# A written order of VectorE, ScalarE and GpSimd for the first block of the second MoE layer, with one weight piece a half

## Chip, cores and metric

One NeuronCore of one Trainium2 chip runs the kernel. The metric is device time in microseconds (us), the median of several runs. Engines: PE is TensorE, DVE is VectorE, ACT is ScalarE, POOL is GpSimd, SP is SyncE, which issues the DMAs here.

## The reference

A windowed attention (with 32 global tokens) is followed by two MoE layers on its 2176 output tokens (4 x 544):

```python
x = attention(q_l, k_l, v_l, q_g, k_g, v_g)      # 2176 tokens x 512
x = layer_norm(solu(x @ w1_in)) * g_ln @ w1_out   # 512 -> 1024 -> 512
h = x @ w2_in                                     # 512 -> 2048
g = where(h >= 1, h, where(h <= -1, 0, (h + 1)**2 / 4))
out = g @ w2_out                                  # 2048 -> 512
```

The inputs `w2_in` and `w2_out` arrive as 64-bit floats. The kernel turns each into two 32-bit numbers, a high and a low part whose sum is the weight, on the chip. Every product is made of three matmuls (high x high, high x low, low x high), which keeps the precision.

## The kernel before

**Stages.** Attention and the first MoE layer come first, up to 309 us. The second layer runs over three blocks of tokens: block 0 (6 tiles of 128 tokens), block 1 (6) and block 2 (5). Its 2048 columns are 16 pieces `f` of 128: for each there is an "i" weight piece (of `w2_in`) and an "o" weight piece (of `w2_out`).

**Block 0, a loop over f = 1 to 15 (line 1084).** A block's tokens are two halves of 384 columns. In this text half k = 2f + (0 or 1). In each half PE makes `h` (`h2`, line 673: 12 matmuls of 384 columns into one PSUM bank of a pool of three, one of which an accumulator takes for good after the first halves), and then 9 matmuls of 512 columns that add piece f - 2 into the six PSUM accumulators (`accum`, line 703; three tiles a half). The activation of a half is `bend` and `least` (lines 688 to 694), then a split in two parts:

- ACT: `relu` (`xy<-h`), then `square` (`xy<-xy`);
- DVE: `least` (`xy<-h,xy`, a minimum and maximum of PSUM and SBUF), after which the PSUM bank is free for the half after next;
- ACT: the high part (`g<-xy`); POOL: the low part (`g<-xy,g`, one instruction of 384 columns).

**A weight piece** is a DMA of 512 KB into one of three buffers `wraw` (`fetch`, line 213) and seven steps (`conv`, line 164): A on ACT (`w<-wraw`), C and B on DVE (`w<-w`), D and F on DVE (`w<-wraw,w`, lines 178 and 180; after F the buffer `wraw` is free), H on ACT (high part, `wo<-w` or `lnT<-w`) and L (low part: DVE here). At the loop's start 19 of the 32 pieces are left. The loop converts two pieces before an odd f and one before an even f (`weights(1 + f % 2, vec)`, line 1086), both pieces step by step together. The "o" pieces live in five rotating buffers (`WO = 5`): piece o(f) takes the buffer of o(f - 5). Each "o" piece is also stored to DRAM (`store_out`) for blocks 1 and 2. `order2` (line 230) sorts the pieces: i(f) by f, o(f) by f + 4.

**What sets the order.** PE and SP follow the written order of the program. In block 0 DVE, ACT and POOL are ordered by the framework's scheduler, within the dependencies (`vec.gate` adds a few). In blocks 1 and 2 (line 1101 on) all engines follow the written order.

**Blocks 1 and 2** make two pieces f at once (`pair`, line 802) by seven products of half the depth (products 0 to 6, of 6 matmuls each) and sums of their results: DVE forms `u1` after product 1 and `u2` after product 3 (lines 829 and 831), and product 4 writes the bank that `u2` reads. The products need sums of weights (`wfull` on POOL, `wsum` on DVE, `whigh` on ACT, `wlow` on POOL, tile `S`) and sums and splits of the tokens (`ysum` on DVE, `yhigh` on ACT, `ylow` on DVE or POOL; tiles `yc` and `yT`). Those that the first pairs of block 1 need are listed in `early` (line 1078) in iterations f = 12 to 15; the scheduler may pull them forward.

**The end of a block.** After the last piece `finish` (line 869) copies each accumulator to SBUF (`o<-acc`, even tiles on ACT, odd ones on DVE) and stores it. Accumulators 0 and 1 are one PSUM tile, 2 and 3 another. A tile is copied right behind its own last matmul, and the framework lets the matmuls of the other accumulator of the same PSUM tile wait for that copy.

## Time and profile before

| | us |
|---|---|
| median of 3 runs | 699.83 |
| the three runs | 699.63, 699.83, 703.38 |
| the profiled execution's own time | 698.82 |
| its span in the trace | 697.0 |
| PE busy | 661.3 (95% of the span) |
| PEld busy | 574.0 (82%) |
| DVE busy | 449.1 (64%) |
| ACT busy | 350.7 (50%) |
| POOL busy | 256.4 (37%) |
| mean granted clock of PE | 0.991 |

The span is what the trace covers; the own time has what lies around it (1.8 us). PE is busy nearly always, but not evenly: the idle time lies at the start, in block 0, at the entry into block 1 and at the very end. In block 0 PE is the engine that all wait for only in some halves, so a share over the whole span says little there.

### The profile page before, as it was taken

To read this page: it belongs to the slowest core of one execution; us is meant where nothing else is said; L and a number is where in the kernel's file an instruction comes from. 1 tells how busy PE (TensorE), PEld (TensorE's weight loads), DVE (VectorE), ACT (ScalarE), POOL (GpSimd) and SP (SyncE) were. 2 spreads that over 40 slices of the span, in tenths; PEclk is the share of its full clock that TensorE was granted. 3 is DMA by queue.
4 is the path that set the end of the run, shared out by engine and by line. 5 is a ranking of instruction groups with operands and counts; after the bars stand their busy time and mean duration, and the time that the engine had idled before them with its cause. 6 is when DMAs were issued, how large, how long until landed. Compare 5 with 4: busy or idle time off the path is not lost.

```text
span 697.0 us, 15054 instructions
## 1 busy us (share of the span) xinstructions
PE 661.3 (95%) x6095; PEld 574.0 (82%) x6095; DVE 449.1 (64%) x800; ACT 350.7 (50%) x859; POOL 256.4 (37%) x275
## 2 busy tenths in 40 slices
PE   5799899999999999999999989989999999999996
PEld 3467788988898898998787778978888888989984
DVE  5999999988777499539755674355555544333332
ACT  4887574354563255344644445544544466444443
POOL 3343633112112143034222247376677645222220
PEclk9999999999999999999999999999999999999999
DMA  8979557435355333002553341555333356644512
GB/s 347 394 257 398 206 185 269 165 127 186 123 217 153 150 92 121 1 0 75 198 151 121 123 149 62 187 171 185 121 121 122 120 182 211 233 130 152 196 46 77
DMA packets 29398, 113.71 MB, mean 163 GB/s; under 512 B 3472, under 2 KB 3984, under 8 KB 26768
## 3 DMA queue, kind: packets, MB, share of 16 engines
q1 hardware_dynamic: 29184, 112.48, 46.0%
q8 instruction: 48, 0.79, 0.5%
q10 hardware_dynamic: 144, 0.26, 0.1%
q14 instruction: 22, 0.18, 0.1%
HBM read 88.87 MB, written 23.86 MB: 162 GB/s over the span
## 4 chain that ended last, share of the span: by engine, by line
PE 67%; DVE 18%; DMA 7%; ACT 3%; issue 3%; POOL 0%; SPq 0%; ACTq 0%; DVEq 0%
PE acc L267 19%; PE h L267 17%; PE h L512 11%; PE yT L267 10%; DVE w L178 3%; DMA wraw<-in_w2o_dram 3%; DVE w L180 3%; DMA wraw<-in_w2i_dram 2%; DVE xy L138 2%; PE S L343 2%; PE plnT L561 2%; PE o L415 2%; PE pPT L400 2%; DVE w L174 1%; DVE e L138 1%
## 5 line engine op out<-in xcount | busy, mean ns | idle before, releaser
L267 PE MATMUL acc<-wo,g 128*128 128x512 f32 x816 | 212.7, 394 | 1.8 <-ACT o L147 1.8
L162 POOL TENSOR_TENSOR g<-xy,g 128x384 fp32r<-128x384 f32 (+1 forms) x95 | 97.2, 1029 | 207.1 <-ACT g L147 163.8
L267 PEld LDWEIGHTS acc<-wo,g 128*128 128x128 f32 x816 | 150.1, 189 | 26.4 <-ACT o L147 2.7
L147 ACT ACTIVATE xy<-xy 128x384 f32<-128x384 f32 (+1 forms) x144 | 72.5, 504 | 71.2 <-DVE xy L138 67.1
L512 PE MATMUL h<-win,x 128*128 128x512 f32 x408 | 102.7, 401 | 0.2 <-DVE x L500 0.2
L267 PE MATMUL yT<-lnT,wout 128*128 128x256 f32 x768 | 94.9, 281 | 0.0
L267 PEld LDWEIGHTS yT<-lnT,wout 128*128 128x128 f32 x768 | 92.3, 188 | 0.8
L512 PEld LDWEIGHTS h<-win,x 128*128 128x128 f32 x408 | 74.4, 188 | 16.8 <-DVE x L500 0.7
L138 DVE TENSOR_TENSOR xy<-h,xy 128x384 f32<-128x384 f32 (+1 forms) x64 | 33.5, 523 | 59.6 <-PE h L267 59.1
L267 PE MATMUL h<-yT,w2i 128*128 128x384 f32 (+1 forms) x300 | 58.6, 342 | 7.1 <-DVE xy L138 4.5
L267 PEld LDWEIGHTS h<-yT,w2i 128*128 128x128 f32 x300 | 52.2, 191 | 13.6 <-DVE xy L138 9.5
L138 DVE SCALAR_TENSOR_TENSOR xy<-h,xy 128x384 f32<-128x384 f32 (+1 forms) x48 | 26.0, 541 | 55.8 <-ACT xy L147 55.8
L147 ACT ACTIVATE g<-xy 128x384 fp32r<-128x384 f32 (+1 forms) x96 | 47.8, 498 | 27.8 <-DVE xy L138 27.6
L147 ACT ACTIVATE xy<-h 128x384 f32<-128x384 f32 (+1 forms) x64 | 30.0, 469 | 51.9 <-PE h L267 51.8
L267 PE MATMUL h<-yT,S 128*128 128x384 f32 (+1 forms) x288 | 54.7, 325 | 0.0
L147 ACT ACTIVATE e<-S,nm 128x128 f32<-128x128 f32 x128 | 45.0, 384 | 18.4 <-DVE nm L138 18.4
L267 PEld LDWEIGHTS h<-yT,S 128*128 128x128 f32 x288 | 48.3, 188 | 5.4 <-DVE xy L138 1.9
L172 ACT ACTIVATE w<-wraw 128x512 f32<-128x512 f32 x33 | 22.1, 673 | 35.4 <-DMA wraw<-in_w2o_dram 21.9
L547 POOL TENSOR_TENSOR rstd<-rstd,nhalf 128x1 f32<-128x1 f32 x17 | 10.8, 633 | 79.1 <-DVE rstd L138 67.6
L267 PE MATMUL h<-yT,lnT 128*128 128x384 f32 (+1 forms) x180 | 34.9, 339 | 5.2 <-DVE xy L138 5.2
L267 PEld LDWEIGHTS h<-yT,lnT 128*128 128x128 f32 x180 | 31.0, 188 | 10.0 <-DVE xy L138 9.2
L500 POOL TENSOR_TENSOR x<-xy,x 128x512 fp32r<-128x512 f32 x16 | 20.7, 1294 | 42.7 <-ACT x L147 42.7
(135 smaller groups left out, 1044.3 us busy)
## 6 DMA issues: line engine op xcount, KB each, us to landing
wo<-w2d_o SPq DMA_DIRECT2D x33, 512.0 KB, 3.3
vw<-in_vwin_dram SPq DMA_DIRECT2D x16, 1024.0 KB, 8.5
qkT<-in_qk_dram SPq DMA_DIRECT2D x16, 832.0 KB, 6.8
wraw<-in_w2i_dram SPq DMA_DIRECT2D x16, 512.0 KB, 4.3
wraw<-in_w2o_dram SPq DMA_DIRECT2D x16, 512.0 KB, 3.9
w2d_s<-S SPq DMA_DIRECT2D x16, 512.0 KB, 5.5
S<-w2d_s SPq DMA_DIRECT2D x16, 512.0 KB, 5.9
w2d_o<-wo SPq DMA_DIRECT2D x15, 512.0 KB, 5.7
```

Of the source, the lines that this page charges most:

```text
L138: self.last = getattr(nc.vector, name)(*args, **kw)
L147: vec.act = nc.scalar.activation(**kw)
L162: eng.tensor_tensor(out=lo, in0=src, in1=hi.bitcast(F32), op=ALU.subtract)
L172: return nc.scalar.activation(out=w.tf, in_=w.high.bitcast(F32), func=AF.Abs)
L178: return nc.vector.scalar_tensor_tensor(out=w.t, in0=w.high, scalar=-0x40000000, in1=w.t, op0=ALU.bitwise_and, op1=ALU.bitwise_or)
L180: return nc.vector.scalar_tensor_tensor(out=w.t, in0=w.low, scalar=29, in1=w.t, op0=ALU.logical_shift_right, op1=ALU.bitwise_or)
L267: mm(out=dst, lhsT=pairs[i][0][x], rhs=pairs[i][1][y], start=start and j == 0, stop=stop and j == 3 * n - 1, **kw)
L343: mm(out=S[32 * hp:32 * hp + 32, par, ci], lhsT=qT[r, hp, ci], rhs=kT[r, hp, w:w + 4].rearrange("p c d -> p (c d)"), start=True, stop=True)
L400: nc.tensor.transpose(ps[:, hp], eT[t][:, HP * par + hp], ident)
L415: mm(out=o[rows, ci, par], lhsT=PT[t][:, par, ci, rows], rhs=w[:, ci, D * h:D * h + D], start=True, stop=True)
L500: eng.tensor_tensor(out=xT[t][1], in0=x[:, :, n:n + P], in1=xT[t][0].bitcast(F32), op=ALU.subtract)
L512: mm(out=hps[t][:, half], lhsT=x[i][:, k], rhs=win[j][:, k, sl], start=not lo and j == 0 and k == 0, stop=lo and k == KD - 1)
```

## The change

- In block 0 too, DVE, ACT and POOL follow a written order. The loop runs over the halves k = 2 to 31 (the first two stand before it). In each half, the order is: `h` on PE; `relu` and `square`; L of the piece before last and C of the last piece on DVE; `least`; A of a new piece on ACT (none in halves 11 and 21, `REST`); B, D, F of the last piece on DVE; the high part of `g`; its low part on POOL, now two instructions of 192 columns; H of the last piece on ACT; the `early` steps of this half; then the 9 accumulating matmuls.
- `order2` sorts o(f) by f + 6 instead of f + 4. All stashed pieces are now "i" pieces, 19 pieces are left for the loop as before, and in the loop the last seven (o9 to o15, halves 15 to 22) follow each other without an "i" piece between them.
- `early` is spread over the halves 24 to 31. The weight sums that block 1 needs first (`wfull`, `wsum`, `whigh`, `wlow`) stand in halves 26 to 31.
- In the first pair of block 1, `yhigh` stands ahead of the other extra steps of its product and `ylow` one product later.
- `finish` copies accumulators 0 and 1 together when both are complete, and 2 and 3 likewise. At the very end accumulator 2 of block 2 is copied by DVE instead of ACT, ahead of accumulator 3 on ACT.

```diff
+REST = (11, 21)
-    order2 = [... for f in range(K2)] + [(f + 4, "o", f) for f in range(K2)])]
+    order2 = [... for f in range(K2)] + [(f + 6, "o", f) for f in range(K2)])]
...
-        lasts = {j: f for f, j in order}
-        return [lambda f=f, j=j: step(f, j, lasts[j] == f) for f, j in order]
+        lasts = {j: (f, j) for f, j in order}
+        done = {at: [] for at in order}
+        for j in range(n):
+            both = [lasts[i] for i in {j, j ^ 1} if i < n and max(j, i) < 4] or [lasts[j]]
+            done[max(both, key=order.index)].append(j)
+        return [lambda f=f, j=j: step(f, j, done[f, j]) for f, j in order]
...
-        if i % 2:
+        if i % 2 or (b, i) == (len(BLOCKS) - 1, 2):
...
-        weights2(16, in_lnr)
+        weights2(18, in_lnr)
-        vec.gate = True
         early = {
-            K2 - 4: [yhigh(1, 0), ylow(1, 0), ysum(1, 0)],
-            K2 - 3: [ysum(1, 1), yhigh(1, 2), ylow(1, 2), ysum(1, 2)],
-            K2 - 2: [yhigh(1, 1), ylow(1, 1), ysum(1, 3)],
-            K2 - 1: [wfull(0, 0), wfull(0, 1), wsum(0, 0..3), whigh(0), wlow(0, 0), wlow(0, 1), wfull(1, 0), wfull(1, 1)],
+            (12, 0): [yhigh(1, 0), ylow(1, 0)],
+            (12, 1): [ysum(1, 0), yhigh(1, 2), ylow(1, 2)],
+            (13, 0): [ysum(1, 1), wfull(0, 0)],
+            (13, 1): [ysum(1, 2), yhigh(1, 1), wfull(0, 1)],
+            (14, 0): [ysum(1, 3), ylow(1, 1)],
+            (14, 1): [wsum(0, 0..3)],
+            (15, 0): [whigh(0), wlow(0, 0), wlow(0, 1)],
+            (15, 1): [wfull(1, 0), wfull(1, 1)],
         }
-        for f in range(1, K2):
-            store_out(3)
-            weights(1 + f % 2, vec)
-            fetch(3 - len(fetched))
-            h2(0, f, 0)
-            if f >= 2:
-                accum(0, f - 2, range(3))
-            h2(0, f, 1)
-            if f >= 2:
-                accum(0, f - 2, range(3, len(BLOCKS[0])))
-            for op in early.get(f, ()):
-                op()
         with tc.manual_schedule(engines={DVE, Activation, Pool}):
+            for k in range(2, 2 * K2):
+                f, half = divmod(k, 2)
+                if half == 0:
+                    store_out(3)
+                fetch(3 - len(fetched) - (piece_now is not None))
+                h, s, gh, gl = hprod(0, f, half)
+                bend(h, s)
+                if piece_low:
+                    conv("L", piece_low, vec)
+                if piece_now:
+                    conv("C", piece_now)
+                least(h, s)
+                piece_next = None
+                if fetched and k not in REST:
+                    make, raw, scale = fetched.pop(0)
+                    piece_next = word(make(), raw, scale)
+                    conv("A", piece_next)
+                if piece_now:
+                    for step in "BDF":
+                        conv(step, piece_now)
+                act(out=gh, in_=s, func=AF.Copy)
+                m = s.shape[1] // 2
+                for sl in (slice(0, m), slice(m, 2 * m)):
+                    sub(gl[:, sl], s[:, sl], gh[:, sl].bitcast(F32), nc.gpsimd)
+                if piece_now:
+                    conv("H", piece_now)
+                piece_low, piece_now = piece_now, piece_next
+                for op in early.get((f, half), ()):
+                    op()
+                if f >= 2:
+                    accum(0, f - 2, range(3) if half == 0 else range(3, len(BLOCKS[0])))
...
-                                extra[i] += [yhigh(1, 3 + i), ylow(1, 3 + i, nc.gpsimd if i % 2 else vec)]
+                                extra[i].insert(0, yhigh(1, 3 + i))
+                                extra[i + 1].insert(0, ylow(1, 3 + i, nc.gpsimd if i % 2 else vec))
```

**DVE in the middle of block 0.** In these rows `h2_...` is the PSUM bank of a half (its row is `least`), `w32_...` a piece in work, `wraw_...` its raw words. Rows of the scalar kind with one `w32` are C, then B; those with `wraw` are D, then F; the last kind is L. Before, f = 9 and 10:

```order
L138 SCALAR_TENSOR_TENSOR xy0_88<-h2_5132,xy0_88 128x384
L174 TENSOR_SCALAR w32_5160<-w32_5160 128x512
L174 TENSOR_SCALAR w32_5162<-w32_5162 128x512
L176 TENSOR_SCALAR w32_5160<-w32_5160 128x512
L176 TENSOR_SCALAR w32_5162<-w32_5162 128x512
L178 SCALAR_TENSOR_TENSOR w32_5160<-wraw_5035,w32_5160 128x512
L178 SCALAR_TENSOR_TENSOR w32_5162<-wraw_5037,w32_5162 128x512
L180 SCALAR_TENSOR_TENSOR w32_5160<-wraw_5035,w32_5160 128x512
L180 SCALAR_TENSOR_TENSOR w32_5162<-wraw_5037,w32_5162 128x512
L138 SCALAR_TENSOR_TENSOR xy0_88<-h2_5180,xy0_88 128x384
L138 TENSOR_TENSOR wo_5159<-w32_5160,wo_5159 128x512
L138 TENSOR_TENSOR lnT1_87<-w32_5162,lnT0_86 128x512
```

And with the change, halves 18 and 19 (the same place in the program):

```order
L177 TENSOR_SCALAR w32_5183<-w32_5183 128x512
L141 SCALAR_TENSOR_TENSOR xy0_88<-h2_5207,xy0_88 128x384
L179 TENSOR_SCALAR w32_5183<-w32_5183 128x512
L181 SCALAR_TENSOR_TENSOR w32_5183<-wraw_5123,w32_5183 128x512
L183 SCALAR_TENSOR_TENSOR w32_5183<-wraw_5123,w32_5183 128x512
L141 TENSOR_TENSOR wo_5182<-w32_5183,wo_5182 128x512
L177 TENSOR_SCALAR w32_5226<-w32_5226 128x512
L141 SCALAR_TENSOR_TENSOR xy0_88<-h2_5246,xy0_88 128x384
```

Two pieces with eight steps stood between two `least` rows; now one piece stands in each half, with three steps behind `least` and two ahead of the next.

**ACT where the last "o" pieces are converted.** `h2_...` marks `relu`, `wo_...<-w32_...` is H of an "o" piece, `w32_...<-wraw_...` is A, `g` the high part. The brackets name what an instruction waits for. Before (o12 and o13 in iteration 11):

```order
L147 ACTIVATE xy0_88<-h2_5323 128x384 [waits PE_49,Pool_49]
L147 ACTIVATE xy0_88<-xy0_88 128x384 [waits Activation_49]
L147 ACTIVATE wo_5303<-w32_5305 128x512 [waits DMAHW2_49,DVE_49]
L147 ACTIVATE wo_5304<-w32_5307 128x512 [waits DMAHW4_49,DVE_49]
L147 ACTIVATE g2_0_4585<-xy0_88 128x384 [waits DVE_49]
```

With the change, from H of o13 (half 20) to `relu` of half 23; `wo_5307` is o14:

```order
L150 ACTIVATE wo_5264<-w32_5265 128x512 [waits DMAHW4_49,DVE_49,PE_49]
L150 ACTIVATE xy0_88<-h2_5326 128x384 [waits Pool_49]
L150 ACTIVATE xy0_88<-xy0_88 128x384 [waits Activation_49]
L150 ACTIVATE g1_0_4388<-xy0_88 128x384 [waits DVE_49]
L150 ACTIVATE wo_5307<-w32_5308 128x512 [waits DMAHW7_49,DVE_49,PE_49]
L150 ACTIVATE xy0_88<-h2_5362 128x384 [waits Pool_49]
L150 ACTIVATE xy0_88<-xy0_88 128x384 [waits Activation_49]
L175 ACTIVATE w32_5380<-wraw_5287 128x512 [waits DMAHW1_49]
L150 ACTIVATE g2_0_4583<-xy0_88 128x384 [waits DVE_49]
L150 ACTIVATE xy0_88<-h2_5394 128x384 [waits Pool_49]
```

H of o12 to o15 now waits for PE too (the matmuls that read the buffer's last owner), and `relu` of the next half stands behind it.

**DVE at the entry into block 1.** `h2_5609`, `h2_5657` are the last half of block 0; `S` rows are `wsum`, `yT` rows `ylow`, `o<-acc` a `finish`, rows from `h2_5666` or `h2_5701` are `u1` and then `u2`. Before:

```order
L138 SCALAR_TENSOR_TENSOR xy0_88<-h2_5609,xy0_88 128x384 [waits Activation_49]
L138 TENSOR_TENSOR yT1_4389<-xy1_89,yT0_4388 128x384 [waits PE_49,Activation_49]
L138 TENSOR_TENSOR yT1_4389<-xy1_89,yT0_4388 128x384 [waits PE_49]
L138 TENSOR_TENSOR xy0_88<-h2_5666,xy0_88 128x384 [waits PE_49,Pool_49]
L138 TENSOR_TENSOR S_5654<-S_5654 128x256
L138 TENSOR_TENSOR S_5654<-S_5654 128x256 [waits DVE_49]
L138 TENSOR_TENSOR yT1_4389<-xy1_89,yT0_4388 128x384 [waits Activation_49]
L138 TENSOR_TENSOR yT1_4389<-xy1_89,yT0_4388 128x384
L138 COPY o_5723<-acc_4691 128x512 [waits PE_49]
L138 SCALAR_TENSOR_TENSOR xy0_88<-h2_5665,xy0_88 128x384
L138 TENSOR_TENSOR xy0_88<-h2_5666,xy0_88 128x384 [waits PE_49]
```

With the change:

```order
L141 SCALAR_TENSOR_TENSOR xy0_88<-h2_5657,xy0_88 128x384 [waits Activation_49]
L141 TENSOR_TENSOR S_5676<-S_5676 128x256 [waits Pool_49]
L141 TENSOR_TENSOR S_5676<-S_5676 128x256 [waits DVE_49]
L141 TENSOR_TENSOR xy0_88<-h2_5701,xy0_88 128x384 [waits PE_49,Activation_49]
L141 TENSOR_TENSOR yT1_4387<-xy1_89,yT0_4386 128x384 [waits Activation_49]
L141 TENSOR_TENSOR yT1_4387<-xy1_89,yT0_4386 128x384
L141 TENSOR_TENSOR S_5676<-S_5676 128x256 [waits DVE_49] x2
L141 COPY o_5754<-acc_4685 128x512 [waits Activation_49]
L141 SCALAR_TENSOR_TENSOR xy0_88<-h2_5700,xy0_88 128x384
L141 TENSOR_TENSOR xy0_88<-h2_5701,xy0_88 128x384 [waits PE_49]
```

All four `wsum` rows now stand behind block 0's last `least`, two of them ahead of `u1`, and the first waits for POOL. The copy of accumulator 1 waits for ACT (its copy of accumulator 0, which stands behind `whigh` of the second pair).

## Rows read from the trace of the kernel before

**Rows 1.** Timeline of PE: start, duration, instruction, idle time before and its releaser.
```profile
318.76 2.35 PE L267 MATMUL h<-yT,w2i 128*128 128x384 f32 x12 [0.46 <-DVE xy L138]
...
428.89 2.27 PE L267 MATMUL h<-yT,lnT 128*128 128x384 f32 x12
...
445.64 1.22 PE L267 MATMUL h<-yc,w2i 128*128 128x384 f32 x6
...
456.69 2.26 PE L267 MATMUL h<-yT,w2i 128*128 128x384 f32 x6 [2.54 <-ACT g L147]
```

**Rows 2.** Waits, 318.76 to 428.89 us: us in total, times, longest.
```profile
ACT w L172 <- DMA wraw<-in_w2o_dram: 15.3, 9, 2.7
...
PE h L267 <- DVE xy L138: 9.2, 16, 1.6
```

**Rows 3.** The chain of waits, 318.76 to 428.89 us, shares by line.
```profile
by line: DMA wraw<-in_w2o_dram 21.4%; DMA wraw<-in_w2i_dram 15.1%; issue 11.0%; DVE w L178 10.6%; DVE w L180 9.5%; DVE xy L138 7.0%; ACT xy L147 5.4%; DVE w L174 4.8%; DVE S L138 2.9%; DVE w L176 2.5%; PE h L267 2.2%; ACT w L172 2.1%; PE ac
```

**Rows 4.** Timeline, one conversion in block 0, all engines (columns as in rows 1).
```profile
373.07 0.66 ACT L172 ACTIVATE w<-wraw 128x512 f32<-128x512 f32 x1 [2.48 <-DMA wraw<-in_w2o_dram]
...
374.70 0.56 DVE L138 SCALAR_TENSOR_TENSOR xy<-h,xy 128x384 f32<-128x384 f32 x1 [3.52 <-ACT xy L147]
...
375.62 0.43 DVE L176 TENSOR_SCALAR w<-w 128x512 int32<-128x512 int32 x1
...
376.08 0.69 DVE L178 SCALAR_TENSOR_TENSOR w<-wraw,w 128x512 int32<-128x512 int32 x1
...
376.44 1.20 POOL L162 TENSOR_TENSOR g<-xy,g 128x384 fp32r<-128x384 f32 x1 [4.39 <-ACT g L147]
376.81 1.38 DVE L180 SCALAR_TENSOR_TENSOR w<-wraw,w 128x512 int32<-128x512 int32 x1
...
378.23 0.63 ACT L147 ACTIVATE lnT<-w 128x512 fp32r<-128x512 f32 x1 [1.54 <-DVE w L180]
```

**Rows 5.** Timeline, an activation with no conversion beside it (half 29).
```profile
435.44 0.49 ACT L147 ACTIVATE xy<-h 128x384 f32<-128x384 f32 x1 [1.99 <-PE h L267]
435.96 0.53 ACT L147 ACTIVATE xy<-xy 128x384 f32<-128x384 f32 x1
436.52 0.56 DVE L138 SCALAR_TENSOR_TENSOR xy<-h,xy 128x384 f32<-128x384 f32 x1 [3.63 <-ACT xy L147]
...
437.77 1.02 POOL L162 TENSOR_TENSOR g<-xy,g 128x384 fp32r<-128x384 f32 x1 [3.17 <-PE h L267]
```

**Rows 6.** Instructions on the tile w2i: count, duration ns min/median/max.
```profile
L763 POOL TENSOR_TENSOR S<-w2i,w2i x20: 729/952/1187, 408.4 to 499.5; 128x256 f32<-128x256 f32 x20
```

**Rows 7.** DMAs from in_w2o_dram, 320 to 450 us.
```profile
DMA to landing us min/median/max: 3.4/4.1/5.5
```

**Rows 8.** Timeline, a weight sum in block 0, then the entry into block 1.
```profile
413.93 0.41 DVE L138 TENSOR_TENSOR S<-S 128x256 f32<-128x256 f32 x1
...
449.86 2.27 DVE L138 TENSOR_TENSOR S<-S 128x256 f32<-128x256 f32 x2
...
452.16 1.06 ACT L147 ACTIVATE S<-S 128x1024 fp32r<-128x1024 f32 x1
...
453.98 1.03 DVE L138 TENSOR_TENSOR yT<-xy,yT 128x384 fp32r<-128x384 f32 x2 [1.86 <-ACT yT L147]
454.93 0.69 DVE L138 COPY o<-acc 128x512 f32<-128x512 f32 x1
...
455.99 0.55 DVE L138 TENSOR_TENSOR xy<-h,xy 128x384 f32<-128x384 f32 x1
```

**Rows 9.** Timeline, the end of block 2.
```profile
685.23 0.58 ACT L147 ACTIVATE o<-acc 128x512 f32<-128x512 f32 x1
...
685.86 5.05 PE L267 MATMUL acc<-wo,g 128*128 128x512 f32 x21 [1.11 <-ACT o L147]
...
691.65 0.96 PE L267 MATMUL acc<-wo,g 128*128 128x512 f32 x3 [0.73 <-ACT o L147]
692.64 0.60 ACT L147 ACTIVATE o<-acc 128x512 f32<-128x512 f32 x1 [1.05 <-PE acc L267]
```

More of the change, by code (lines that the diff above doesn't have):

```diff
@@ L1074 @@
         S[1].append(m1.tile([P, 4, 2, P], F32R, tag="e", name="S1_1", bufs=3))
-        vec.gate = True
         early = {
-            K2 - 4: [lambda: yhigh(1, 0), lambda: ylow(1, 0, nc.gpsimd), lambda: ysum(1, 0)],
-            K2 - 3: [lambda: ysum(1, 1), lambda: yhigh(1, 2), lambda: ylow(1, 2, nc.gpsimd), lambda: ysum(1, 2)],
-            K2 - 2: [lambda: yhigh(1, 1), lambda: ylow(1, 1, nc.gpsimd), lambda: ysum(1, 3)],
-            K2 - 1: [lambda: wfull(0, 0), lambda: wfull(0, 1), *(lambda i=i: wsum(0, i) for i in range(4)), lambda: whigh(0), lambda: wlow(0, 0), lambda: wlow(0, 1), lambda: wfull(1, 0), lambda: wfull(1, 1)],
-        }
@@ L1098 @@
-        g4 += [gring[1], g3, gring[2], gring[0]]
-        banks += [psA.tile([P, 512], F32, tag="A", name="h2") for _ in range(2)]
+            (12, 0): [lambda: yhigh(1, 0), lambda: ylow(1, 0, nc.gpsimd)],
+            (12, 1): [lambda: ysum(1, 0), lambda: yhigh(1, 2), lambda: ylow(1, 2, nc.gpsimd)],
+            (13, 0): [lambda: ysum(1, 1), lambda: wfull(0, 0)],
+            (13, 1): [lambda: ysum(1, 2), lambda: yhigh(1, 1), lambda: wfull(0, 1)],
+            (14, 0): [lambda: ysum(1, 3), lambda: ylow(1, 1, nc.gpsimd)],
@@ L1100 @@
+            (14, 1): [lambda i=i: wsum(0, i) for i in range(4)],
+            (15, 0): [lambda: whigh(0), lambda: wlow(0, 0), lambda: wlow(0, 1)],
+            (15, 1): [lambda: wfull(1, 0), lambda: wfull(1, 1)],
+        }
+        piece_now = piece_low = None
         prev[0] = 0, K2 // 2 - 1
         with tc.manual_schedule(engines={mybir.EngineType.DVE, mybir.EngineType.Activation, mybir.EngineType.Pool}):
+            for k in range(2, 2 * K2):
[29 more added lines that the diff above has]
+                    accum(0, f - 2, range(3) if half == 0 else range(3, len(BLOCKS[0])))
+            assert not (todo or fetched or piece_now or piece_low)
+            store_out(0)
+            g3 = [stg.tile([P, 1024], I32, tag="wraw", name=f"g3_{i}").bitcast(F32R)[:, :BT] for i in range(2)]
+            g4 += [gring[1], g3, gring[2], gring[0]]
+            banks += [psA.tile([P, 512], F32, tag="A", name="h2") for _ in range(2)]
```

22 lines of the change are left out of this document (12 added, 10 removed).

## Prediction, made before the change was timed

> **What bounds the kernel now.** I read the page first (PE is busy 95% of the span), then the timeline of PE alone through block 0 [rows 1]. The last four halves of block 0 (k = 28 to 31) have no conversions left beside them: they run from 428.89 to 445.64, that is 4.19 us a half, with no gap. This is what a half costs when PE is the bound. The 27 halves from k = 5 (318.76) to the end of block 0 (445.64) took 126.9 us; at 4.19 they would take 113.1. So **13.8 us** are lost in block 0. A gap of 2.54 follows at the entry into block 1 (456.69), and two of 1.11 and 0.73 at the very end [rows 9].
>
> The waits tell who is late in block 0 [rows 2]: PE waits 16 times for DVE's `least`, which frees the PSUM bank, and ACT waits for the raw words of a piece to land (15.3 us for the "o" pieces alone). The chain of waits says how these hang together [rows 3]: the two DMAs hold 36% of it, DVE's conversion lines some 27%, PE's `h` 2%. The path is DMA, A on ACT, the activation behind A, `least`, the rest of the conversion on DVE, a freed buffer, the next DMA. One link of it is shown in the timeline [rows 4]: ACT sits idle 2.48 us for the landing, runs A at 373.07, and `least` starts only at 374.70. The reader should see that conversions are on the path because they stand in front of `least` on ACT and DVE.
>
> **The change part by part.** Durations are of the profiled execution (698.82 us, span 697.0); its sum is then moved to the median, which is 1.0 us higher.
>
> *Conversions leave the path: minus 13.8.* No conversion step is removed: 19 pieces with seven steps each remain, with their 19 loads and 16 stores. What moves is where they stand. A piece's A now runs a half ahead of its C, B, D, F, and H and L follow later, so nothing in a half's own activation needs that half's landing in order to go on. I checked three resources for what becomes the bound.
>
> (a) The landing. A buffer is freed by F, about 6 us into a half (below), and is next needed by A two halves later, 8.4 + 3.4 = 11.8 us into the same count. This leaves 5.8 us for a landing of 4.1, at most 5.5 [rows 7]. SP issues the loads in order with the stores ahead of them; those wait for L steps that are long done. Hidden, with 0.3 us to spare at worst.
>
> (b) The ring through ACT and DVE. In the written order `relu` of a half stands behind H of the last piece, H needs F, F stands behind `least`, and `least` needs `relu`. One turn is H 0.63 [rows 4], `relu` 0.52 and `square` 0.56 from start to start [rows 5], `least` 0.56, B 0.46 and D 0.73 from start to start, F 0.69 (taken as long as D; its own row of 1.38 has a wait in it) [rows 4]: together 4.15, just under 4.19. POOL's low part comes on top where it gets between D and F: in rows 4 POOL's instruction started at 376.44 while D ran, and F took 1.38 instead of 0.69. POOL's pieces are now 192 columns wide, a size that the trace doesn't have; from 1.02 for 384 columns [rows 5] and 0.73 for 256 [rows 6] I estimate 0.58 on a straight line. The ring is then 4.15 with no piece in it, 4.73 with one, 5.31 with both. It need not fit into 4.19 at once: `least` of a half ends 4.0 us after its `h` began (433.08, one half after 428.89, to 437.08 [rows 1, 5]) and the bank is wanted after two halves, at 8.38, which is 4.4 us to spare. Halves 11 and 21 take no new piece, and so the half behind them has no B, D, F, H and catches up; there are eight or nine halves between. With one piece the ring falls behind by 0.54 a half, 4.3 us in eight halves, within the 4.4. I take **0** for it: the two pieces are separate instructions, DVE's D or F goes between them, and one of the two most likely falls on `least`, which was 0.56 in rows 4 and 5 alike. The bound on the other side is both pieces: 1.12 x 8 - 4.4 = 4.6 us twice, 9.2.
>
> The Trainium skill has a rule that speaks against the change here (SBUF — State Buffer, section "Who interferes with whom"): a VectorE instruction with two inputs in SBUF and a GpSimd instruction that reads SBUF exclude each other, and the first holds the shared ports for its whole length. Rows 4 agree (F 1.38 beside POOL, D 0.69 just before). By the rule alone both pieces can stand in the ring, which is the rival below with 9.2 us more.
>
> *Later "o" pieces: plus 4.6.* H of o(f) writes the buffer of o(f - 5), so it must wait for the accumulating matmuls of o(f - 5), in halves 2(f - 3) and 2(f - 3) + 1. The order by f + 6 puts H of o12 to o15 in halves 19, 20, 21 and 23, and their buffers are free at the end of halves 19, 21, 23 and 25. ACT stands still meanwhile, with `relu` of the next half behind it. For o12 this costs nothing (F ends later anyway). For o13, `relu` of half 21 waits to the end of half 21, and `least` of 21 is done 2.3 us later, when half 23 wants its bank only after 4.2. For o14 ACT waits to the end of half 23, and half 24 wants the bank of half 22, whose `relu` stands behind that H: PE waits for H 0.53, `relu` 0.52, `square` 0.56, `least` 0.56 and some 0.1 of handing over, **2.3 us**. For o15 the same at the end of half 25: 2.3 more. No row of before has this wait (H of o15 waited for PE there too, but nothing stood close behind it). Bounds: 0, if the bank came free earlier than I count, and 9.2, if all four stop PE. I take 4.6 by the count of halves.
>
> *Entry into block 1: plus 1.5 (0.3 to 2.7).* Call its start T (445.64 before). Product 4 started at T + 11.05, when it could have at T + 8.5. The scheduler had pulled `early` forward; now POOL has, one behind the other: the low part of half 30 (ready at T - 3.7 by rows 5), `wlow` 4 x 0.73, the low part of half 31 and `wfull` of the second pair 4 x 0.73 to 0.95 [rows 6], to T + 4.6 to 5.5. DVE's first `wsum` waits for it, and behind it in DVE's queue stand `wsum` again (0.41 each alone, 1.14 each with POOL beside it), `u1` 0.55, `ylow` 1.03 and two more `wsum`: T + 7.8 to 10.2. Then `whigh` on ACT 1.06 and, behind it, ACT's copy of accumulator 0, 0.58; DVE's copy of accumulator 1 waits for that, 0.69; then `least` and `u2`, 0.55 each [rows 8, 9]. Product 4 starts at T + 11.3 to 13.7. I take T + 12.5, as POOL has `ylow` to do right after `wfull` and so is beside `wsum`.
>
> *Copies in pairs: minus 1.8, plus 0.7.* At the end PE no longer waits for copies of the neighbour accumulator: 1.11 and 0.73 are gone [rows 9]. What is late next there is the data of piece 31 (its last low part on DVE ended at 686.0), which is wanted some 2 us later than the matmuls released: hidden. But the last two copies now stand in a row, DVE 0.69 [rows 8] and then ACT 0.60 [rows 9], where there was one ACT copy: plus 0.7. At the other block ends PE didn't wait for a copy, so nothing is won.
>
> Attention and the first MoE layer keep their instructions; only which pieces are stashed and loaded differs, in equal sizes, and SP is far ahead there: 0.
>
> *Sum:* -13.8 + 0 + 4.6 + 1.5 - 1.8 + 0.7 = **-8.8**: own time 690.0, median **691.0**.
>
> **The rivals.**
>
> *Both POOL pieces stand in the ring* (and the rests clear it): 9.2 more, **700.2**. For it: the rule above, and a ring that without POOL is already 4.15 of 4.19. Against it: it needs POOL to win the ports twice in each half between `least` and the end of F, while DVE's next step is ready at once.
>
> *The same, and the rests don't clear it* (slower): a resting half saves B, D, F and H of one piece, 2.5 us, but if ACT is by then behind on `relu`, `square` and A as well, the backlog stays. Then 17 halves lose 1.12 each, less the 4.4 once: 14.6 more, **705.6**. It decides against the change from a ring of 4.19 + (8.8 + 4.4) / 17 = 5.0 us.
>
> *The buffers of the "o" pieces stop no one:* 4.6 less, **686.4**. For it: each stop hangs on one bank and a margin of 2 us. Against it: the order puts H two halves ahead of its buffer.
>
> *The change doesn't do what it says* (A still waits for landings): were they 7 us, three halves would hold 7.0 + A 0.67 + a half 4.2 + B, D, F 2.4 = 14.3, or 4.76 a half, some 5 us in all, 696. No landing in rows 7 is so long, so it has no chance of its own and lies in the range.
>
> **How the numbers follow.** 0.5% of 699.83 is 3.5 us, about what a measurement can tell from no change: faster is below 696.3, slower above 703.3. Forecast 0.73 (its own range 688 to 696: entry from 0.3 to 2.7, and a ring of up to 5.0, which gives 2 x 2.1 us), "o" buffers free 0.08, both pieces 0.12 (no change), both pieces without rests 0.07 (slower). Faster is 0.73 + 0.08 = 0.81, same 0.12, slower 0.07. The range from 686.0 to 698.0 holds the forecast, the rival below it and the longer landings, and leaves out 0.19.
>
> **What would show it.** In the changed kernel's timeline of PE, halves start every 4.19 us from k = 5 to 23 with no wait for DVE; block 1 starts near 436. There are two gaps of about 2.3 us, at halves 24 and 26, and in ACT's row before each an H of `wo` that waited for PE `acc`. Product 4 starts 12 to 13 us behind block 1's start. PE has no wait for ACT's `o` at the end, and the last ACT copy follows a DVE copy. If waits of PE for `least` recur through halves 8 to 20, the ring was too long; if halves 24 and 26 start on time, the count of buffers was wrong. A block 1 that starts later than 442 would make the sum wrong in its main term.

## The result, and the profile after

The changed kernel took 693.38 us in the median (691.32 to 695.33, 4 runs) beside 700.87 us of the kernel before (699.63 to 703.38, 4 runs): a ratio of 0.989, 95% interval 0.984 to 0.994. Its profiled execution took 691.32 us with a span of 689.5 us, 7.50 us less than the profiled execution of before (698.82). Forecast were 8.8 us less and a median of 691.0. The time lies in the range, on the side that was forecast.

The timeline of PE in the changed kernel (start, duration, instruction, idle time before and its releaser) answers [rows 1]:

```profile
321.45 2.27 PE L270 MATMUL h<-yT,w2i 128*128 128x384 f32 x12
...
396.81 2.27 PE L270 MATMUL h<-yT,lnT 128*128 128x384 f32 x12
...
403.48 2.35 PE L270 MATMUL h<-yT,lnT 128*128 128x384 f32 x12 [2.32 <-DVE xy L141]
...
414.42 2.37 PE L270 MATMUL h<-yT,lnT 128*128 128x384 f32 x12 [2.31 <-DVE xy L141]
...
439.64 1.22 PE L270 MATMUL h<-yc,w2i 128*128 128x384 f32 x6
...
447.06 1.63 PE L270 MATMUL h<-yT,S 128*128 128x384 f32 x6 [1.34 <-DVE xy L141]
...
452.02 1.28 PE L270 MATMUL h<-yT,w2i 128*128 128x384 f32 x6 [1.94 <-ACT g L150]
```

From half 5 (321.45) to half 23 (396.81) a half starts every 4.19 us with no gap: 75.36 us for 18 halves. Then PE stands twice, in front of half 24 (403.48) and of half 26 (414.42). Block 1 starts at T = 439.64, product 3 at T + 7.4 and product 4 at T + 12.4.

What PE waits for at half 24 stands in the timeline of ACT and DVE just ahead:

```profile
401.20 0.63 ACT L150 ACTIVATE wo<-w 128x512 fp32r<-128x512 f32 x1 [5.59 <-PE acc L270]
401.74 0.47 ACT L150 ACTIVATE xy<-h 128x384 f32<-128x384 f32 x1
...
402.24 0.52 ACT L150 ACTIVATE xy<-xy 128x384 f32<-128x384 f32 x1
...
402.87 0.56 DVE L141 SCALAR_TENSOR_TENSOR xy<-h,xy 128x384 f32<-128x384 f32 x1 [0.31 <-ACT xy L150]
```

H of o14 has waited 5.59 us for the accumulating matmuls of o9; `relu`, `square` and `least` follow one by one, and `least` releases PE. The waits of the whole stretch (321.45 to 439.64; us in total, times, longest) show the same three pieces, and no wait of ACT for a weight DMA, where [rows 2] had 15.3 us for the "o" pieces alone:

```profile
ACT wo L150 <- PE acc L270: 13.5, 3, 6.0
```

The entry into block 1, all engines:

```profile
441.21 2.83 POOL L769 TENSOR_TENSOR S<-w2i,w2i 128x256 f32<-128x256 f32 x4
...
444.08 2.37 DVE L141 TENSOR_TENSOR S<-S 128x256 f32<-128x256 f32 x2 [4.62 <-POOL S L769]
...
446.37 0.55 DVE L141 TENSOR_TENSOR xy<-h,xy 128x384 f32<-128x384 f32 x1
...
448.68 1.06 ACT L150 ACTIVATE S<-S 128x1024 fp32r<-128x1024 f32 x1 [1.84 <-DVE S L141]
...
449.64 0.58 ACT L150 ACTIVATE o<-acc 128x512 f32<-128x512 f32 x1
...
450.25 0.69 DVE L141 COPY o<-acc 128x512 f32<-128x512 f32 x1 [1.61 <-ACT o L150]
...
451.33 0.55 DVE L141 TENSOR_TENSOR xy<-h,xy 128x384 f32<-128x384 f32 x1
```

DVE waits 4.62 us for POOL's `wfull`, does two `wsum` in 2.37 us and only then `u1` (446.37), for which product 3 waits. Then come `whigh`, ACT's copy, DVE's copy behind it, and `u2` (451.33), for which product 4 waits.

The end (answers [rows 9]): the last 20 matmuls run without a gap, and the last two copies stand in a row, DVE and then ACT.

```profile
679.70 4.70 PE L270 MATMUL acc<-wo,g 128*128 128x512 f32 x20
...
684.44 0.69 DVE L141 COPY o<-acc 128x512 f32<-128x512 f32 x1 [2.76 <-PE acc L270]
685.16 0.60 ACT L150 ACTIVATE o<-acc 128x512 f32<-128x512 f32 x1 [1.49 <-DVE o L141]
```

The mean granted clock of a stretch (columns: stretch, its length, busy time of PE, PEld, DVE, ACT, POOL with counts, granted clock, DMA share, GB/s), first behind the gap of 2.54 us at product 4 in the kernel before, then behind the gap at half 24 in the changed one:

```profile
456.69:459.00 2.31, 2.31 (x7) 2.31 (x8) 0.02 (x1) 1.16 (x2) 2.23 (x3) 0.50 0.34 127
```

```profile
403.48:407.75 4.27, 4.27 (x21) 3.88 (x22) 2.85 (x5) 1.93 (x4) 2.69 (x4) 1.00 0.00 0
```

In the kernel before, PE ran behind that gap at 0.50, its 1.2 GHz level: the six matmuls of product 4 took 2.26 us where those of another product took 1.22 [rows 1]. In this trace of the changed kernel no gap was followed by that, the one of 1.94 us at product 4 included (1.28 us for its six matmuls).

**Where the 7.5 us went**, from the timelines of the two profiled executions:

| stretch | before | changed | difference | forecast |
|---|---|---|---|---|
| start to half 5 | 318.76 | 321.45 | +2.69 | 0 |
| half 5 to T (27 halves) | 126.88 | 118.19 | -8.69 | -13.8 + 4.6 |
| T to product 4 | 11.05 | 12.38 | +1.33 | +1.5 |
| product 4 to product 4 of block 1's last pair (569.70, then 563.55) | 113.01 | 111.53 | -1.48 | 0 |
| from there to the end of the span | 127.30 | 125.95 | -1.35 | -1.8 + 0.7 |
| sum | 697.0 | 689.5 | -7.5 | -8.8 |

### The profile page after: what moved, and what is told of

Read it like the earlier page. It is cut to its first block, busy times and chain, and to the rows that moved or that the text cites. A ratio compares the mean times of both kernels' runs of the same rounds, so it can differ in the third digit from the quotient of the medians.

```text
span 689.5 us, 15113 instructions
## 1 busy us (share of the span) xinstructions
PE 657.3 (95%) x6095; PEld 575.3 (83%) x6095; DVE 445.7 (65%) x801; ACT 351.4 (51%) x858; POOL 270.4 (39%) x305
## 4 chain that ended last, share of the span: by engine, by line
PE 79%; DVE 13%; ACT 3%; issue 2%; POOL 1%; DMA 1%; SPq 0%; DVEq 0%; POOLq 0%; ACTq 0%
PE acc L270 26%; PE h L270 24%; PE h L515 10%; PE yT L270 9%; PE plnT L564 2%; DVE nm L141 2%; DVE w L181 2%; PE o L418 2%; PE S L346 2%; PE pPT L403 2%; DVE w L183 2%; DVE e L141 2%; DVE xy L141 1%; DVE S L141 1%; ACT e L150 1%
## 5 line engine op out<-in xcount | busy, mean ns | idle before, releaser
L165 POOL TENSOR_TENSOR g<-xy,g 128x384 fp32r<-128x384 f32 (+1 forms) x65 | 62.3, 966 | 135.3 <-ACT g L150 108.7
L747 POOL TENSOR_TENSOR g<-xy,g 128x192 fp32r<-128x192 f32 x60 | 50.3, 859 | 61.4 <-ACT g L150 56.6
L270 PE MATMUL h<-yT,w2i 128*128 128x384 f32 (+1 forms) x300 | 56.5, 335 | 2.1 <-ACT g L150 1.9
```

The source lines that it names most:

```text
L165: eng.tensor_tensor(out=lo, in0=src, in1=hi.bitcast(F32), op=ALU.subtract)
L270: mm(out=dst, lhsT=pairs[i][0][x], rhs=pairs[i][1][y], start=start and j == 0, stop=stop and j == 3 * n - 1, **kw)
L747: eng.tensor_tensor(out=out, in0=x, in1=y, op=ALU.subtract)
```

## The experiments

All stretches in one table, each from the timeline of PE of one profiled execution (us). A fall of the granted clock to 0.50 lengthens the stretch that it lies in by some 1.5 us; how often that was, behind the start of block 0, is in the last column.

| kernel | half 0 starts | half 5 to T | T to product 4 | T to the end of the last matmul | falls of the clock |
|---|---|---|---|---|---|
| before | 299.49 | 126.88 | 11.05 | 246.97 | 1 |
| before, again (`e10`) | 299.94 | 127.41 | 11.04 | 246.84 | 1 |
| changed | 302.80 | 118.19 | 12.38 | 244.76 | 0 |
| changed, again (`e8`) | 299.13 | 119.76 | 12.36 | 244.76 | 1 |
| `e1` third rest | 304.52 | 113.04 | 12.37 | 246.08 | 1 |
| `e2` sums late | 300.43 | 119.76 | 9.49 | 246.17 | 1 |
| `e3` low part in one | 299.63 | 125.15 | 12.28 | 244.76 | 2 |
| `e4` copies as before | 301.04 | 121.32 | 10.67 | 245.69 | 2 |
| `e5` third rest, pairs at the end only | 301.29 | 113.04 | 10.67 | 243.14 | 0 |
| `e6` as `e5`, sums behind u1 | 300.43 | 113.04 | 9.46 | 244.63 | 1 |
| `e7` two pieces | 300.95 | 116.74 | 12.36 | 246.03 | 1 |
| `e9` two raw buffers | 302.75 | 113.04 | 12.36 | 244.66 | 0 |
| `e11` A ahead of relu | 299.46 | 118.53 | 12.36 | 244.81 | 0 |
| `e12` the same, two buffers | 301.00 | 118.55 | 12.37 | 246.04 | 1 |

**Is it the buffers of the "o" pieces (`e1`)?**

```diff
-REST = (11, 21)
+REST = (11, 12, 21)
```

> The changed kernel with one more half without a new piece (half 12), so that every later piece is converted one half later; nothing else differs. My theory: the two gaps of PE in front of halves 24 and 26 (2.32 and 2.31 us) come from the high parts of o14 and o15, which wait on ACT for the matmuls of o9 and o10 at the ends of halves 23 and 25 while the next relu stands behind them. One half later the waiting is as long at most, but the relu behind it belongs to a half whose PSUM bank is wanted 4.2 us later and not at once: both gaps vanish, block 0 takes 113.2 to 113.6 us from half 5 instead of 118.2, and the kernel is 4.6 us faster than the changed one. Rival (the turn of ACT and DVE is too long, its spare time is used up by half 24, and a rest at half 21 comes too late): a rest at half 12 clears the backlog of the first ten halves alone, so the two gaps stay within some 0.5 us of 2.3 each and the time within 1 us.

687.65 us (4 runs), ratio to before 0.982 (0.977 to 0.986). Both gaps are gone, and 27 halves take 113.04 us, 5.15 less; the prediction's floor was 113.1. In its timeline halves 24 and 26 start on time (PE), and H of the last "o" piece still waits 3.75 us for PE (ACT), with no consequence:

```profile
402.71 2.27 PE L270 MATMUL h<-yT,lnT 128*128 128x384 f32 x12
...
411.09 2.27 PE L270 MATMUL h<-yT,lnT 128*128 128x384 f32 x12
411.29 0.63 ACT L150 ACTIVATE wo<-w 128x512 fp32r<-128x512 f32 x1 [3.75 <-PE acc L270]
```

So the wait itself costs nothing; it costs when the `relu` behind it belongs to a half whose bank is wanted at once. The rival, a long turn, would have left the gaps.

**The entry: sums out of the way (`e2`).** `at` numbers the products at which sums of the next pair, high part and low parts stand (the edit is shortened).

```diff
-extra[0] += [wsum(p + 1, 0), wsum(p + 1, 1)]
-extra[1] += [wsum(p + 1, 2), wsum(p + 1, 3)]
-extra[2], extra[3], extra[4] += whigh, wlow 0, wlow 1
+at = (3, 3, 4, 4, 5) if p == 0 else (0, 1, 2, 3, 4)
+extra[at[0]], extra[at[1]] += sums 0 and 1, sums 2 and 3
+extra[at[2]], extra[at[3]], extra[at[4]] += whigh, wlow 0, wlow 1
```

> The changed kernel, but in the first pair of block 1 the four weight sums for the second pair stand behind u2 on DVE (product 3 instead of 0 and 1), and their high and low parts one to two products later. My theory: of the entry's 3.9 us (product 4 at T + 12.38 where matmuls alone would let it start at T + 8.5) all is due to DVE's queue: the first weight sum waits for POOL until T + 4.4, and u1, the copy, least and u2 stand behind it. With the sums out of the way product 3 starts with no wait (1.34 us before) and product 4 at T + 8.5 to T + 9.5; 2.9 to 3.9 us faster. Rival (POOL and ACT are as late as DVE: low parts of the tokens, the copies in pairs): product 4 still starts behind T + 11. A second rival: the second pair now waits for its sums, which come later, and a gap of 1 to 3 us stands in front of its product 1, so that the total changes by less than 1 us.

694.99 us (8 runs), ratio to before 0.991 (0.988 to 0.994): not faster than the changed kernel. Product 3 has no wait and product 4 starts at T + 9.49, as the theory says. But the gain is given back, by the second rival, in product 3 of the second pair:

```profile
455.76 1.44 POOL L747 TENSOR_TENSOR S<-S,S 128x256 fp32r<-128x256 f32 x2 [3.80 <-ACT S L150]
...
463.22 2.33 DVE L141 TENSOR_TENSOR S<-S 128x256 f32<-128x256 f32 x2 [2.01 <-POOL S L769]
465.47 0.55 DVE L141 TENSOR_TENSOR xy<-h,xy 128x384 f32<-128x384 f32 x1
...
466.07 1.33 PE L270 MATMUL h<-yT,S 128*128 128x384 f32 x6 [3.25 <-DVE xy L141]
```

The later sums made the high part on ACT later, for which POOL waited 3.80 us, and with it POOL's low parts and its next `wfull`. DVE waits for that again, and `u1` stands behind it again.

**The split of the low part (`e3`).**

```diff
-for sl in (slice(0, m), slice(m, 2 * m)):
-    sub(gl[:, sl], s[:, sl], gh[:, sl].bitcast(F32), nc.gpsimd)
+sub(gl, s, gh.bitcast(F32), nc.gpsimd)
```

> The changed kernel with POOL's low part of a half in one instruction of 384 columns again instead of two of 192. In the changed kernel one turn of ACT and DVE takes 4.34 us, since F takes 0.97 beside POOL instead of 0.69. My theory: one long instruction of POOL holds D or F for most of its length; the turn becomes 4.6 to 4.85, 0.4 to 0.65 us per half are lost against 4.19, and after the spare 4.4 us are used PE waits for least: 0 to 1 us before each rest, 0 to 2 us in all, with waits of PE for DVE between halves 8 and 22 if it is near the upper end. Rival (the split decides nothing, since two pieces follow each other without a gap): the turn stays 4.3 to 4.4 and no wait appears.

695.44 us (7 runs), ratio to before 0.993 (0.990 to 0.996). The mechanism is as expected, its price was not. One turn in the changed kernel, and then in this one (from `least` to `least`):

```profile
376.77 0.56 DVE L141 SCALAR_TENSOR_TENSOR xy<-h,xy 128x384 f32<-128x384 f32 x1
...
377.70 0.69 DVE L181 SCALAR_TENSOR_TENSOR w<-wraw,w 128x512 int32<-128x512 int32 x1
377.97 1.90 POOL L747 TENSOR_TENSOR g<-xy,g 128x192 fp32r<-128x192 f32 x2 [2.44 <-ACT g L150]
...
378.43 0.98 DVE L183 SCALAR_TENSOR_TENSOR w<-wraw,w 128x512 int32<-128x512 int32 x1
...
381.11 0.56 DVE L141 SCALAR_TENSOR_TENSOR xy<-h,xy 128x384 f32<-128x384 f32 x1
```

```profile
378.30 0.55 DVE L141 SCALAR_TENSOR_TENSOR xy<-h,xy 128x384 f32<-128x384 f32 x1
...
379.54 1.24 POOL L747 TENSOR_TENSOR g<-xy,g 128x384 fp32r<-128x384 f32 x1 [3.43 <-ACT g L150]
...
379.94 1.39 DVE L183 SCALAR_TENSOR_TENSOR w<-wraw,w 128x512 int32<-128x512 int32 x1
...
382.98 0.55 DVE L141 SCALAR_TENSOR_TENSOR xy<-h,xy 128x384 f32<-128x384 f32 x1
```

The turn is 4.34 us with two short pieces and 4.68 with one long one; F takes 0.98 and 1.39, where D takes 0.69. PE begins to wait at half 10. The 4.4 us of spare time were there at half 3 only, whose `least` ended 3.9 us after its `h` began. Half 4 began 2.1 us behind half 3, since no accumulating matmuls stand between them, and its `least` was 6.5 us behind its `h`; from there the lag grew by 0.49 us a half to 8.5 at half 8, whose bank half 10 wants. 27 halves take 125.15 us, 6.96 more, of which two falls of the clock are some 3.0 (the half behind a gap takes 5.68 and 5.83 us here, and 4.27 to 4.29 without a fall). Some 4 us are thus waits, where I had expected 0 to 2 in all.

**The copies one by one (`e4`).**

```diff
-both = [lasts[i] for i in {j, j ^ 1} if i < n and max(j, i) < 4] or [lasts[j]]
-done[max(both, key=order.index)].append(j)
+done[lasts[j]].append(j)
...
-if i % 2 or (b, i) == (len(BLOCKS) - 1, 2):
+if i % 2:
```

> The changed kernel with the accumulators copied out one by one, as before the change. My theory: at the very end PE waits again for ACT's copies (1.1 and 0.7 us), and the last two copies no longer stand in a row (0.7): the last stretch, from the second half of block 2 on, is 1.1 to 1.4 us longer. At the entry into block 1 the copies of accumulators 0 and 1 no longer wait for each other; product 4 starts up to 0.6 us earlier. Sum: 0.5 to 1.4 us slower. Rival (the paired copy is what holds product 4 back): product 4 starts 1 us or more earlier and the kernel is no slower.

692.16 us (4 runs), ratio to before 0.988 (0.984 to 0.992), the same as the changed kernel. There are two effects of opposite sign: product 4 starts at T + 10.67 instead of T + 12.38, 1.7 us earlier where my theory had at most 0.6 and the rival 1 or more, and PE's two waits at the end are back:

```profile
679.95 5.05 PE L270 MATMUL acc<-wo,g 128*128 128x512 f32 x21 [1.10 <-ACT o L150]
685.74 0.96 PE L270 MATMUL acc<-wo,g 128*128 128x512 f32 x3 [0.74 <-ACT o L150]
```

From T to product 4 of block 1's last pair this kernel is 1.1 us shorter than the changed one (122.8 to 123.9), from there to the end 1.5 longer (127.5 to 126.0). The paired copies pay at the end and cost at the entry.

**Both together (`e5`).** The third rest, and pairs in block 2 alone:

```diff
-REST = (11, 21)
+REST = (11, 12, 21)
...
-both = [lasts[i] for i in {j, j ^ 1} if i < n and max(j, i) < 4] or [lasts[j]]
+both = [lasts[i] for i in {j, j ^ 1} if i < n and max(j, i) < 4 and (b == len(BLOCKS) - 1 or i == j)] or [lasts[j]]
```

> The changed kernel with the third rest (half 12), and with accumulators copied out in pairs in block 2 alone, one by one in blocks 0 and 1. My theory: the two edits touch different stretches and add up. Halves 24 and 26 start with no gap (27 halves in 113.1 to 113.5 us), and at the entry DVE's copy of accumulator 1 no longer stands behind whigh and ACT's copy: product 4 starts at T + 10.7 as with the copies of before, not at T + 12.4. At the end nothing changes against the changed kernel. 5.5 to 6.5 us faster than the changed kernel in the stretch from half 5 to the end. Rival (the copies of block 0 and those at the end hang together, or the gap at product 4 returns at the next pair): no more than 4.6 us.

681.87 us (681.40 to 683.83, 4 runs) beside 699.61 of before: ratio 0.973 (0.968 to 0.977), the fastest kernel of this study, some 11.5 us below the changed one's median. From half 5 to the end of the last matmul it takes 356.18 us, the changed one 362.95: 6.8 less, slightly above the 6.5 expected. The other 4.7 us between the medians are not shown by these two traces. The changed kernel has three gaps of 1.9 us or more behind which the clock can fall, `e5` has none.

**The sums behind u1 (`e6`),** on top of `e5`: `at = (1, 3, 4, 4, 5) if p == 0 else (1, 1, 2, 3, 4)` in the notation of `e2`.

> The kernel of the run before (third rest, pairs in block 2 alone), with DVE's weight sums for the next pair moved behind u1: in the first pair of block 1 two of them directly behind u1 and two behind u2, in the later pairs all four behind u1. The high and low parts follow a product later in the first pair. My theory: the sums wait for POOL's wfull, and u1 stands behind them, in the first pair and in the second too; with u1 ahead of them product 3 starts with no wait in both, product 4 at T + 8.5 to T + 9.7, and no gap above 0.5 us is left in the first two pairs: 1.5 to 2.7 us faster than the run before from T to the end. Rival (POOL is the limit of the first pairs: the sums come late whatever stands ahead of them): a gap of 1 to 3 us moves to the second or third pair and the time stays within 0.7 us.

684.25 us (4 runs), ratio to before 0.976 (0.972 to 0.980): slower than `e5` by some 2 us. The wait moves, as the rival said, though the loss is more than its 0.7 us: product 4 of the first pair starts 1.2 us earlier, and product 4 of the second waits behind four sums that waited for POOL. The clock fell there, too (granted 0.67 over the 2 us behind the gap). The rival's reason, that POOL itself is the limit, is not shown. POOL stood idle for 2.89 us before its low parts, for the high part on ACT, which the edit had moved two products later, and its next `wfull` followed them. As in `e2`, the move itself made POOL late.

```profile
448.12 1.44 POOL L747 TENSOR_TENSOR S<-S,S 128x256 fp32r<-128x256 f32 x2 [2.89 <-ACT S L150]
...
455.51 3.29 DVE L141 TENSOR_TENSOR S<-S 128x256 f32<-128x256 f32 x4 [2.16 <-POOL S L769]
...
459.79 1.74 PE L270 MATMUL h<-yT,w2i 128*128 128x384 f32 x6 [2.24 <-DVE xy L141]
```

**Two pieces in every second half (`e7`).**

```diff
-REST = (11, 21)
+REST = (10, 12)
...
-if fetched and k not in REST:
+while fetched and half == 0 and k not in REST and len(piece_next) < 2:
```

(and C, B, D, F, H and L for each of the two)

> The changed kernel with the written order kept but two weight pieces in every second half instead of one in each (rests at halves 10 and 12, so that the buffers of the o pieces are as late). Theory one, mine: what took the conversions off the path is one piece a half with its A a half ahead, since a freed buffer then has 5.8 us to be filled. With two at a time both buffers come free at the end of an odd half and are wanted by A in the next: A waits 4 to 5 us for the landing and the conversions of two pieces stand in one turn; block 0 is 15 to 40 us longer, with waits of ACT for in_w2i and in_w2o back. Theory two: it is the written order of DVE and ACT (least ahead of B, D and F) that does it, whatever the number of pieces: block 0 stays within 2 us.

689.81 us in one run. My theory falls: 27 halves take 116.74 us, 3.7 more than with one piece a half and no gap (113.04), not 15 to 40. Theory two's 2 us hold beside the changed kernel (118.19, with its two gaps) and not beside that floor. PE waits six times for `least`, 0.23 to 0.42 us each; one of them:

```profile
351.11 2.37 PE L270 MATMUL h<-yT,w2i 128*128 128x384 f32 x12 [0.37 <-DVE xy L141]
```

I had overlooked that the third buffer always holds a landed piece: only one load had to land between F and A, and no wait of ACT for a DMA shows. The written order carries most of the gain (10.1 us of 126.88 - 113.04 = 13.8), whether pieces come singly or in twos.

**The changed kernel again (`e8`)** and **the kernel before again (`e10`)**:

> The changed kernel once more. Up to the first half of block 0 all kernels here have the same instructions in the same order on every engine, and yet that half started at 299.5 to 304.5 us in the six traces so far, and behind the gaps of 2.3 us at halves 24 and 26 the granted clock was 1.00 in one trace and 0.5 in others. My theory: both are scatter of one and the same program, so this trace will differ from the first one of the changed kernel in one or both: first half of block 0 between 299 and 305, and behind each gap a half of either 4.3 or 5.8 us. Everything between (halves of 4.19 us, gaps of 2.3 us, product 3 at T + 7.4, product 4 at T + 12.4) stays within 0.1 us. Rival (the changed weight order slows the first 300 us by 3.3 us): the start of block 0 stays at 302.5 to 303.

> The kernel before once more, for what scatters in it. My theory: the start of its first half of block 0 lies anywhere from 299 to 305 us, as in the traces of the changed kernel, and the gap of 2.5 us in front of product 4 is followed by a half-speed clock or not; the 27 halves of block 0 take 126.9 us within 0.5, and product 4 starts at T + 11.05. Rival: the start stays at 299.5, so that the changed kernel does lose 2 to 3 us before block 0.

`e8`: 693.32 us (4 runs), ratio to before 0.989 (0.983 to 0.994), its profiled execution 689.22. Half 0 starts at 299.13, 3.67 us earlier than in the first trace of the same kernel, so the +2.69 of the table lies within the scatter of one kernel, and the rival of `e8` falls. The two gaps are 2.31 us again; behind the first the clock fell this time, behind the second not:

```profile
399.80:405.66 5.86, 5.86 (x21) 5.26 (x22) 2.86 (x5) 1.94 (x4) 3.04 (x4) 0.71 0.00 0
412.33:416.60 4.27, 4.27 (x21) 3.88 (x22) 1.09 (x2) 3.54 (x7) 3.69 (x6) 1.00 0.00 0
```

The two executions differ by 3.67 less 1.57 = 2.10 us, which is 691.32 - 689.22. `e10` took 699.69 in one run: half 0 at 299.94, and 127.41 and 11.04 for the two stretches. Both traces of before thus start half 0 below 300 us, as the rival of `e10` said, and the other twelve start it at 301.1 in the mean, so a price of some 1 us ahead of block 0 is not excluded.

**Putting the suspected waits back (`e9`, `e11`, `e12`).** All three with the third rest.

```diff
-fetch(3 - len(fetched) - (piece_now is not None))
+fetch(2 - len(fetched) - (piece_now is not None))
```

> The changed kernel with the third rest (as in the first experiment), and with at most two raw pieces in flight or in work in block 0 instead of three: the load of a piece is issued only after the half in which the piece before it has been read for the last time. It puts the suspected wait of the kernel before back (A on ACT, in front of relu, waits for a landing) and leaves the written order and the instructions as they are. My theory: the landing on the path is what cost block 0 of the kernel before its 13.8 us. A load then lands in the same half in which A wants it: F of one half, 4.1 us of landing, A 0.66, and g, H, relu, square, least, B, D, F of the next one 4.9 us make 9.6 us for two halves instead of 8.4. 27 halves take 3 to 10 us more than with three buffers (113.0), with waits of ACT for in_w2i and in_w2o of 1 to 3 us and of PE for least. Rival (order and place on DVE and ACT alone decide, landings are hidden anyway): within 1 us.

686.12 us in one run, 113.04 us for 27 halves. The rival's number, but the edit was empty: in its timeline a load is issued right behind F of the piece that had the buffer, as with three, since that is all that SP waits for.

```profile
350.23 0.98 DVE L183 SCALAR_TENSOR_TENSOR w<-wraw,w 128x512 int32<-128x512 int32 x1
...
351.27 0.33 SPq L220 DMA_DIRECT2D wraw<-in_w2o_dram  x1
```

It moved the load in SP's written order and took no buffer away, so it says nothing of landings.

`e11`, then `e12` (which adds the edit of `e9`):

```diff
+conv("A", piece_next)
 bend(h, s)
...
 least(h, s)
-conv("A", piece_next)
```

> The changed kernel with the third rest, three raw buffers as usual, and one step moved: A of the new piece stands ahead of the half's relu on ACT instead of behind square. My theory after the last runs: what cost block 0 of the kernel before its 13.8 us is the place of the conversion on ACT, ahead of relu, and with it everything that A waits for. Here the raw words have landed, so A costs its own 0.66 us in the turn of ACT and DVE: 4.9 to 5.0 us instead of 4.34, 0.7 to 0.8 us a half over 17 halves, less the spare time of 3.5 us once or twice: 27 halves take 5 to 10 us more than 113.0, with waits of PE for least. Rival (the place of A doesn't matter, the scheduler's pairs of pieces did): within 1 us.

> The same with two raw buffers. With A behind square the second and third buffer made no difference (113.04 us for 27 halves with three and with two). My theory: that is so because relu and square of the next half fill the time of the landing; with A ahead of relu the landing stands in the turn: F, landing 3.6 to 4.1, A 0.66, relu 0.52, square 0.56, least 0.56, B 0.46, D 0.73, F 0.97 make 8.1 to 8.6 us for each half that takes a piece instead of 4.19, so 27 halves take 50 to 75 us more, with waits of ACT for in_w2i and in_w2o of 3 us or more in each. Rival (landings are early, their cost in the kernel before came from the pairs): no more than in the run with three buffers.

`e11`: 688.78 us in one run; 118.53 us for 27 halves, 5.5 more than 113.04, in the expected 5 to 10. Halves that wait for `least` come every 4.90 us:

```profile
340.59 2.35 PE L270 MATMUL h<-yT,w2i 128*128 128x384 f32 x12 [0.44 <-DVE xy L141]
...
345.49 2.35 PE L270 MATMUL h<-yT,w2i 128*128 128x384 f32 x12 [0.46 <-DVE xy L141]
```

One step of 0.66 us ahead of `relu` thus costs 5.5 us here, with no landing to wait for, beside the 13.8 us that block 0 lost before. `e12` (691.11 us in one run) took 118.55, the same, because its edit was as empty as that of `e9`; the 50 to 75 us of my theory there rested on it.

## Why the prediction was right, and where it was not

- **Conversions leave the path (-13.8): right.** Halves 5 to 23 of the changed kernel start every 4.19 us, and with the two gaps out of the way (`e1`) all 27 take 113.04 us, against 113.1 in the sum. The reason given, that conversions stood ahead of `least` on ACT and DVE, is shown in part: A alone ahead of `relu`, with one piece a half, costs 5.5 us (`e11`). How the rest divides between landings that ACT waited for and steps of two pieces between two `least` stays open, since no run took a landing's cover away. A further part was not the conversions alone. Halves 24 to 27 of the kernel before (408.81 to 428.89) hold 3.3 of the 13.8 us, and there the scheduler had put weight sums of `early` among the conversions on DVE (rows of `S`; the rows of `xy` are `least`). No run separates that share:

```profile
413.26 0.41 DVE L138 TENSOR_TENSOR S<-S 128x256 f32<-128x256 f32 x1
...
414.27 0.55 DVE L138 SCALAR_TENSOR_TENSOR xy<-h,xy 128x384 f32<-128x384 f32 x1
...
415.67 1.23 DVE L138 TENSOR_TENSOR S<-S 128x256 f32<-128x256 f32 x1
...
419.25 0.54 DVE L138 SCALAR_TENSOR_TENSOR xy<-h,xy 128x384 f32<-128x384 f32 x1
```

- **(a) The landing: right.** The load issued at 375.13 is wanted by the A at 380.91, 5.8 us later as counted, and no wait of ACT for a DMA is left.
- **(b) The ring: 0 was right, by a turn of 4.34 us,** between the 4.15 of no POOL piece in it and the 4.73 of one. The two pieces alone took 1.16 us together, 0.58 each, the size estimated. The rival with both pieces (5.31) did not come. The reason given was half right: F (378.43 to 379.41) ended before POOL's second piece (379.87), so it waited for the first alone, but no piece fell on `least` (381.11). The spare time was set too large: of its 4.4 us, some 2.2 were gone at half 4 (`least` 6.1 us behind its `h`), which the count from half 29 could not show. At 0.15 us a half that made no difference. With one whole piece in the ring, which the sum took for harmless, it would not have been 0: at 4.68 us a turn PE waits from half 10 on (`e3`). The rule of the Trainium skill (SBUF — State Buffer, section "Who interferes with whom"), that the later of the two instructions waits until the earlier has ended, agrees with these rows: in `e3`, F is longer than D by 0.70 us, in the changed kernel by 0.29, as POOL's instruction is long or short.
- **Later "o" pieces (+4.6): the right mechanism, at the right halves, undersized.** H of o13, o14 and o15 wait, and those of o14 and o15 stop PE. With the slower start of the halves behind the gaps the price is 5.15 us, and 1.57 more for each fall of the clock, which the sum had not.
- **Entry (+1.5 at product 4, T + 12.5): right in size (T + 12.38),** with two parts of its chain misjudged. `u1` also holds product 3 (1.34 us), and the pairing of the copies alone is 1.7 us of the delay (`e4`). The sum had `whigh`, ACT's copy and DVE's copy one behind the other in its chain, but did not tell that the pairing is what puts them there.
- **The clock at the entry (-1.48): a missed term.** The row of product 4 stood in my first group with 2.26 us for six matmuls beside others of 1.22. I counted the gap of 2.54 and not the half-speed stretch behind it. It is no gain that the change is sure of: the changed kernel still has a gap of 1.94 us there, and in the eight traces with a gap of 1.93 to 1.97 us at product 4 the clock fell behind three (`e1`, `e7`, `e12`).
- **Copies at the end (-1.8 + 0.7): right,** -1.35 measured.
- **Ahead of block 0 (0): not contradicted, and not shown.** The two traces of the changed kernel start half 0 at 302.80 and 299.13, those of before at 299.49 and 299.94.

So the sum came within 1.3 us of the measured difference partly by luck: a fall of the clock that this trace was spared (-1.48) and the scatter of the first 300 us (+2.69) worked against each other. The rivals fell: PE had no wait for `least` from half 5 to 23, and the "o" buffers did stop PE.
